# A linear attention and its routed experts: k scaled by cos with its relu, v and v*tan joined by one strided operand, all row writes on VectorE, and w1 loaded later

## The chip, the cores and the metric

The kernel runs on one core of a Trainium2 chip. The time is the device time of one launch, in microseconds; the figure of a kernel is the median of its runs. Engines are written as in the profile: PE is TensorE's matmul, PEld its weight load, DVE is VectorE, ACT is ScalarE, POOL is GpSimd, SP is SyncE. "L586" is line 586 of the kernel before.

## The reference

Two stages follow one another. The first is an attention without softmax, over 8 batches of 8 heads, 576 tokens and a head width of 64. Each token has an angle, theta, that grows with its position; `c` and `s` are its cosine and sine.

```python
def phi(x, c, s):
    r = np.maximum(x, 0.0)
    return np.concatenate([r * c, r * s], axis=-1)
q_p = phi(q, cos_w, sin_w)
k_p = phi(k, cos_w, sin_w)
kv = np.einsum('bhsf,bhsd->bhfd', k_p, v)
z = np.sum(k_p, axis=2)
num = np.einsum('bhsf,bhfd->bhsd', q_p, kv)
den = np.einsum('bhsf,bhf->bhs', q_p, z)[..., None] + 1e-06
return (num / den).astype(np.float32)
```

The 4608 resulting rows of 512 then go through a mixture of 8 experts:

```python
logits = x @ w_gate
expert_idx = np.argmax(logits, axis=1)
...
gate_w = probs[np.arange(N), expert_idx]
for i in range(N):
    e = expert_idx[i]
    if counts[e] < capacity:
        disp[e, counts[e]] = x[i]
...
h = np.maximum(np.einsum('ecd,edf->ecf', disp, w1), 0.0)
y = np.einsum('ecf,efd->ecd', h, w2)
...
        out[i] = gate_w[i] * y[expert_idx[i], pos[i]]
```

Each row takes one expert; w1 is 512 x 1024 and w2 1024 x 512 for each expert, and an expert takes at most 1152 rows.

## The kernel before

**Planner.** The kernel does not issue its work as it is written. Every piece of work is an `op` with an engine, an assumed cost, the data it reads and writes, the buffers it uses (`Ver`, a version that takes one of a fixed number of `Slots`) and a priority. `Plan.schedule` simulates the engines with those costs and fixes one order; `emit` writes the instructions in that order. `PHI` adds an offset to the priorities by kind of op. On the chip each engine runs its own list strictly in this order and waits wherever an input is late; the planner's costs say nothing of what the chip takes.

**Attention, for each batch.** `load` (L405, on SP's queue) brings v, k and q in two halves `u` of four heads each, 576 KB a load; a batch is six loads. `scale_v` (L433 on ACT, L435 on DVE) makes `vs`, which holds v times cos and v times sin for each of nine token groups `j`: 18 instructions a batch. `relu_k` (L419, in batch 0 L421) and `q_relu` (L458) clip k and q. `kv_half` (L504, the op KV) multiplies k by vs in tiles of 64x64 and sums over the tokens into PSUM. The result is copied twice by ACT: `kvt` (L516), which PE transposes (L533, op T), and `kva` (L521). The transposed copy `tsb` (L538) is multiplied with the gate weights `wg_sb` (L547, op G), and the products join `kva` (L552), so that one matmul later gives numerator, denominator and gate logits at once. q is transposed on PE (L468) and copied to `rq` (L475). The op P (L574), ten units a batch, multiplies `rq` by `kva`; each output row holds the cos part and the sin part. ACT copies the cos part to `tmp` (L581), and DVE adds tan of the position times the sin part (L586) to make `num`. Three PSUM buffers (`p`) pass from P to `tmp` and `num`.

**Routing, for each batch.** A chain of small DVE instructions (L627 to L735) makes the reciprocal of the denominator, the logits, the chosen expert (`oh`), its weight and, with counting matmuls on PE (L693 to L700) and a running `carry`, the place of each row; POOL adds a small number at L667. Then the five row groups of the batch are scaled and rounded to bf16 (`f_emit`, L758): groups 1 and 3 on POOL, 0, 2 and 4 on DVE. POOL scatters each group to DRAM with an indirect DMA (L767).

**Experts.** 43 blocks of 128 rows: a block is fetched (L967), transposed (L976), copied (`xT`, L982 on ACT or L984 on DVE), multiplied by one half of w1 (`up`, L999), clipped (`relu`, L1006), transposed back (L1014), copied (`hT`, L1020), and, after all blocks, multiplied by w2 (`down`, L1040), copied (`y`, L1046 and L1048) and scattered to the output (L1057). 20 blocks are taken from the first six batches, so that they can begin while the last batches are still at work. w1 and w2 are loaded by POOL's queue, which turns fp32 into bf16 on the way: the first half of w1 (`w1a`, L918) in eight loads that follow the KV of batches 0 to 5, the second half (`w1b`) and w2 after the attention has freed its memory.

The gate of the w1 loads is this line:

```python
w1_load(0, e, e + 0.1, ops_of("KV", 3 * e // 4))
```

Of the kernel before, what the change touches and what calls it, by code (L numbers as in the profile page):

```python
# [20 lines left out]
P = 128  # L21
DISJOINT = "the rows written are disjoint"
# [5 lines left out]
    "KV": 0.67, "P": 1.53, "Q": 1.08, "R": 0.18, "T": -0.18, "carry": 0.52, "count": -1.68, "down": 0.08,  # L28
    "end": 0.57, "fetch": 1.92, "gout": -0.13, "hT": 0.05, "ix": -0.43, "kvt": -0.86, "num": 0.22,
    "pad": -1.04, "pos": -0.01, "pre": -0.23, "relu": 0.14, "reluk": -0.5, "reluq": -1.78, "rq": -0.43,  # L30
    "seen": 0.24, "tab": 0.85, "tmp": 0.34, "tsb": 0.47, "turn": 5.12, "up": 2.21, "vs": -0.73, "w1": 0.14,
    "w2": 0.51, "wg": -1.23, "xg": 0.06, "xturn": -0.12,
# [25 lines left out]
class Plan:  # L58
# [6 lines left out]
    def op(self, eng, cost, fn, r=(), w=(), vers=(), prio=0.0, lat=0.1, mode=None, dma=0.0, after=()):  # L65
        o = Op()
        o.eng, o.cost, o.fn, o.prio, o.lat, o.mode, o.dma = eng, cost, fn, prio, lat, mode, dma
        o.seq, o.start, o.end = len(self.ops), None, None
# [18 lines left out]
    def schedule(self, window=0.25, switch=0.15, sticky=0.6):  # L87
# [11 lines left out]
        while done < len(self.ops):  # L99
            best = {}  # L100
            cands = []
            for o in ready:
                t = max(free.get(o.eng, 0.0), o.avail)
# [17 lines left out]
                if o.mode is not None and mode.get(o.eng) not in (None, o.mode):  # L121
                    t += switch
                cands.append((t, o))
                if o.eng not in best or t < best[o.eng]:
                    best[o.eng] = t
# [4 lines left out]
            eng = min(best, key=lambda e: best[e])  # L130
            t0 = best[eng]
            pick = None
            for t, o in cands:
                if o.eng == eng and t <= t0 + window:
                    pr = o.prio - (sticky if o.mode is not None and mode.get(eng) == o.mode else 0.0)
                    if pick is None or (pr, o.seq) < pick[0]:
                        pick = ((pr, o.seq), t, o)
            _, t, o = pick
# [29 lines left out]
    def emit(self):  # L168
        for o in self.order:
            o.fn()  # L170
# [3 lines left out]
def kernel(  # L174
# [11 lines left out]
    nc = tc.nc  # L186
# [24 lines left out]
    XT_ACT = 14  # L211
# [35 lines left out]
    kS, vS, qS = Slots("km", 4), Slots("vm", 2), Slots("qm", 2)  # L247
    qrS = Slots("qr", 2)
    vsS, rqS, kvaS = Slots("vs", 2), Slots("rq", 2), Slots("kva", 2)
    tmpS = Slots("tmp", 3)  # L250
    kvtS, tsbS, numS = Slots("kvt", 1), Slots("tsb", 1), Slots("num", 2)
# [6 lines left out]
    vs_t = [early.tile([P, HB, J, 2, D + 1], FP32, name=f"vs{i}") for i in range(vsS.n)]  # L258
# [23 lines left out]
    for t in range(2):  # L282
        nc.gpsimd.dma_start(out=wg_n[t * D:(t + 1) * D], in_=moe_w_gate.rearrange("(h d) e -> d h e", d=D))
# [16 lines left out]
    nc.scalar.activation(out=cosn[:], in_=tok_n[:], func=ACT.Sin, bias=halfpi[:])  # L300

# [20 lines left out]
    for t, tab in ((0, cosn), (1, sinn)):  # L322
      for vs in vs_t:
        nc.gpsimd.tensor_copy(out=vs[:, :, :, t, D], in_=tab[:].unsqueeze(1).to_broadcast([P, HB, J]))
    for t_ in num_t:
        nc.gpsimd.memset(t_[D:P, NJ, :, :], 1.0)

    nc.gpsimd.memset(wg_sb[:], 0.0)

    def wg_spread():  # L330
        for t in range(2):
            rows = slice(t * D, (t + 1) * D)
            for o in range(2):
                nc.gpsimd.tensor_copy(out=wg_sb[rows, 2 * o:2 * o + 2, t, :, :],
                                      in_=wg_n[rows].rearrange("p (u c o) e -> p o u c e", u=2, c=2)[:, o])
# [54 lines left out]
    def load(b, name, u):  # L390

        if name == "v":
            if u == 0:
                loaded[b, "v"] = Ver(vS)
            vm = loaded[b, "v"]
        else:
            vm = loaded[b, name, u] = Ver({"k": kS, "q": qS}[name])
        src = srcs[name][b].rearrange("(u c o) (p j) d -> u (o p) c (j d)", u=2, o=2, j=J)[u]

        def f():  # L400
            if name == "v":
                m = tl(vm, [P, HB, J, D], FP32, "early")[:, 2 * u:2 * u + 2, :, :]
            else:
                m = tl(vm, [P, 2, J, D], FP32, "early")[:]
            nc.sync.dma_start(out=m.rearrange("p c j d -> p c (j d)"), in_=src)  # L405
        op("SP", 0.5, f, w=[(name, b, u)], vers=[vm], prio=b - 1.2, dma=1.55).tag = ("load", name, b, u)
# [3 lines left out]
    def attention(b):  # L410

        vm = loaded[b, "v"]
        pr = float(b)

        def relu_k(u):
            def f():
                kk = loaded[b, "k", u].tile[:]
                if b:
                    nc.scalar.activation(out=kk, in_=kk, func=ACT.Relu)  # L419
                else:  # L420
                    nc.vector.tensor_scalar(out=kk, in0=kk, scalar1=0.0, scalar2=None, op0=ALU.max)  # L421
            return f


        vs = Ver(vsS)

        def scale_v(j, t, us):
            def f():
                tab = (cosn, sinn)[t]
                heads = slice(2 * us[0], 2 * us[-1] + 2)  # L430
                dst, src = vs_t[vs.slot][:, heads, j, t, 0:D], vm.tile[:, heads, j, :]
                if on_act(j):
                    nc.scalar.activation(out=dst, in_=src, func=ACT.Copy, scale=tab[:, j:j + 1])  # L433
                else:
                    nc.vector.tensor_scalar(out=dst, in0=src, scalar1=tab[:, j:j + 1], scalar2=None, op0=ALU.mult)  # L435
            return f

# [738 lines left out]
```

## Time and profile before

| | before |
|---|---|
| median of 3 runs | 396.09 us (395.18 to 398.47) |
| the profiled execution | 398.65 us |
| its span in the profile | 396.6 us |
| mean granted TensorE clock | 0.932 |
| busy: PE, DVE, ACT, POOL | 336.3, 210.2, 188.9, 154.3 us |

The span is what the profile's engines cover; the execution's own time lies 2.05 us above it. A row of a group reads: line, engine, operation, output and inputs with their shapes, count, then busy time and mean ns of one, then the engine's idle time before these instructions and what ended it. A row of waits reads: the waiting engine and line, what it waited for, total us, number of times, longest. Two rows of the same engine can overlap, as ACT and DVE start the next instruction before the last has ended: the means of the rows are longer than the distance from start to start.

### The profile page before, as it was taken

How to read it: one execution, taken by the hardware profiler on the slowest of the kernel's cores; microseconds unless marked ns; L12 is line 12 of the kernel's file. 1: busy time of each engine (PE TensorE's matmuls, PEld its weight loads, DVE VectorE, ACT ScalarE, POOL GpSimd, SP SyncE). 2: the span in 40 equal slices, each digit the busy share in tenths (PEclk: the TensorE clock that was granted, in tenths of full speed). 3: DMA queues.
4: the chain of work that ended last, by engine and by line, in shares of the span. 5: the costliest groups of instructions: out<-in, count | busy, mean ns of one | idle time of the engine just before them, and what ended most of it. 6: DMA issues, size and time to landing. Idle time of an engine off the chain costs nothing.

```text
span 396.6 us, 9673 instructions
## 1 busy us (share of the span) xinstructions
PE 336.3 (85%) x3368; PEld 221.2 (56%) x3368; DVE 210.2 (53%) x584; ACT 188.9 (48%) x403; POOL 154.3 (39%) x214
## 2 busy tenths in 40 slices
PE   6588698878897996788397787899999999999992
PEld 3477597757686875674254343455555544444440
DVE  6547878796867697878725333444333311222220
ACT  5576776777675695547063232345555311111110
POOL 6100546454653627084723222105000065555552
PEclk9978986999797799989879998999999999999998
DMA  8999787778979501126599997819920033342330
GB/s 271 335 341 311 246 248 225 240 223 260 259 221 229 197 3 62 45 71 147 172 202 236 202 213 146 176 47 165 211 51 2 1 134 159 139 162 110 126 129 1
DMA packets 38543, 66.63 MB, mean 168 GB/s; under 512 B 3903, under 2 KB 18655, under 8 KB 38498
## 3 DMA queue, kind: packets, MB, share of 16 engines
q0 software_dynamic: 18096, 31.00, 34.5%
q1 hardware_dynamic: 19250, 33.98, 26.1%
q10 hardware_dynamic: 1152, 1.05, 0.8%
q8 instruction: 29, 0.48, 0.5%
q14 instruction: 16, 0.13, 0.1%
HBM read 67.56 MB, written 17.06 MB: 213 GB/s over the span
## 4 chain that ended last, share of the span: by engine, by line
PE 44%; DVE 15%; DMA 12%; issue 11%; POOL 6%; ACT 5%; POOLq 2%; ACTq 2%; SPq 1%; DVEq 0%
PE p L999 17%; PE p L574 9%; PE p L1040 7%; POOL out_dram L1057 6%; DMA xr<-xd 5%; DMA vm<-in_v_dram 5%; PE a L1014 4%; DVE xg L758 4%; DVE num L586 3%; PE a L468 3%; DMA qm<-in_q_dram 2%; POOLq L1057 2%; ACT tmp L581 2%; PE a L976 2%; PE a L547 1%
## 5 line engine op out<-in xcount | busy, mean ns | idle before, releaser
L1006 ACT ACTIVATE h<-p 128x512 bf16<-128x512 f32 x86 | 51.3, 598 | 63.3 <-PE p L999 61.7
L1040 PE MATMUL p<-w,un 128*128 x344 | 74.6, 379 | 0.3 <-issue 0.3
L574 PE MATMUL p<-kva,rq 64*128 64x146 f32 x640 | 61.2, 345 | 13.9 <-DVE num L586 10.9
L1020 DVE COPY un<-a 128x512 bf16<-128x512 bf16 x86 | 36.0, 423 | 63.5 <-PE a L1014 63.3
L574 PEld LDWEIGHTS p<-kva,rq 64*128 64x128 f32 x640 | 53.1, 229 | 21.8 <-DVE num L586 14.5
L1040 PEld LDWEIGHTS <-un 128*128 128x128 bf16 x344 | 33.6, 98 | 40.6 <-issue 0.6
L586 DVE SCALAR_TENSOR_TENSOR num<-p,tant,tmp 128x292 f32<-128x292 f32 (+1 forms) x80 | 39.8, 516 | 24.4 <-ACT tmp L581 19.2
L767 POOL DMA_INDIRECT xd<-xg,si x40 | 47.1, 1178 | 11.1 <-issue 8.8
L999 PEld LDWEIGHTS <-un 128*128 128x128 bf16 x344 | 32.7, 99 | 30.5 <-issue 9.5
L999 PE MATMUL p<-w1a,un 128*128 x172 | 46.7, 399 | 2.5 <-POOL ids L971 0.5
L581 ACT COPY tmp<-p 128x292 f32<-128x292 f32 (+1 forms) x80 | 31.2, 402 | 35.3 <-PE p L574 25.8
L1048 DVE COPY y<-p 128x512 f32<-128x512 f32 x22 | 15.2, 691 | 57.7 <-PE p L1040 51.9
L999 PE MATMUL p<-w1b,un 128*128 x172 | 44.1, 378 | 0.0
L1057 POOL DMA_INDIRECT out_dram<-y,ids x20 | 19.5, 976 | 58.5 <-DVE y L1048 46.8
L504 PE MATMUL p<-vs,km 64*64 64x130 f32 x1152 | 34.6, 272 | 9.1 <-DVE km L421 4.3
L1046 ACT COPY y<-p 128x512 f32<-128x512 f32 x21 | 12.3, 586 | 61.2 <-PE p L1040 61.2
L504 PEld LDWEIGHTS p<-vs,km 64*64 64x64 f32 x1152 | 32.1, 133 | 11.2 <-issue 5.2
L1014 PEld LDWEIGHTS <-h 128*128 128x128 bf16 x344 | 25.2, 99 | 22.5 <-ACT h L1006 10.0
L1014 PE MATMUL a<-identb,h 128*128 128x128 bf16 x344 | 33.5, 222 | 4.9 <-ACT h L1006 4.2
L758 POOL TENSOR_TENSOR xg<-num,rden 128x512 bf16<-128x512 f32 x16 | 24.0, 1520 | 18.4 <-DVE rden L735 18.4
L971 POOL COPY ids<-xr 128x2 bf16<-128x2 bf16 x43 | 7.6, 190 | 56.6 <-DMA xr<-xd 56.3
L468 PE MATMUL a<-ident,qr 128*128 128x128 f32 x144 | 27.3, 319 | 2.1 <-ACT rq L475 1.8
(162 smaller groups left out, 405.2 us busy)
## 6 DMA issues: line engine op xcount, KB each, us to landing
vm<-in_v_dram SPq DMA_DIRECT2D x16, 576.0 KB
km<-in_k_dram SPq DMA_DIRECT2D x16, 576.0 KB
qm<-in_q_dram SPq DMA_DIRECT2D x16, 576.0 KB
w<-in_moe_w_dram POOLq DMA_DIRECT2D x16, 512.0 KB
xr<-xd SPq DMA_DIRECT2D x43, 128.5 KB
w1a<-in_moe_w_dram POOLq DMA_DIRECT2D x8, 512.0 KB
w1b<-in_moe_w_dram POOLq DMA_DIRECT2D x8, 512.0 KB
xd<-zrow ACTq DMA_DIRECT2D x8, 128.5 KB
```

The costliest lines, as they stand in the source:

```text
L468: nc.tensor.transpose(out=q_ps[:, n * P:(n + 1) * P], in_=qr.tile[:, j, :, :].rearrange("p c d -> p (c d)"), identity=ident[:])
L504: nc.tensor.matmul(out=kv_v[c * D:(c + 1) * D, o, u, :, :], lhsT=loaded[b, "k", u].tile[o * D:(o + 1) * D, c, j, :], rhs=vs_t[vs.slot][o * ...
L574: nc.tensor.matmul(out=p_ps[:, a, o, 0:2 * KW], lhsT=rq[u].tile[a * D:(a + 1) * D, o, col:col + P], rhs=kva.tile[a * D:(a + 1) * D, o, u, ...
L581: nc.scalar.copy(out=t[0:rows], in_=p_v[0:rows, :, 0:KW])
L586: nc.vector.scalar_tensor_tensor(out=num.tile[0:rows, c, u * HB:(u + 1) * HB, :], in0=p_v[0:rows, :, KW:2 * KW], scalar=tant[0:rows, c:c + ...
L758: eng.tensor_tensor(out=x[0:rows, c, 0:DT].rearrange("p (h d) -> p h d", h=H), in0=num.tile[0:rows, c, :, 0:D], in1=rv["rden"][0:rows, c, ...
L767: si = nc.gpsimd.indirect_dma_start(out=xd[:, :], out_offset=bass.IndirectOffsetOnAxis(ap=xg.si[0:rows, c:c + 1], axis=0), in_=xg.tile[0:r ...
L999: nc.tensor.matmul(out=hp, lhsT=xv.tile[:, g, :], rhs=w1h[m][:, bass.ds(e1, 1), g, :], start=(g == 0), stop=(g == G - 1))
L1006: nc.scalar.activation(out=h[:], in_=pvs[m].tile[:, 0, :].rearrange("p (g q i) -> p g i q", g=2, i=2), func=ACT.Relu)
L1014: nc.tensor.transpose(out=t_ps[:, x * P:(x + 1) * P], in_=hvs[m].tile[:, x // 2, x % 2, :], identity=identb[:])
L1040: nc.tensor.matmul(out=y_ps, lhsT=hts[x // G].tile[:, x % G, :], rhs=w2h[x // G][:, bass.ds(e2, 1), x % G, :], start=(x == 0), stop=(x == ...
L1057: oi = nc.gpsimd.indirect_dma_start(out=out[:, :], out_offset=bass.IndirectOffsetOnAxis(ap=idx, axis=0), in_=yv.tile[:], in_offset=None, b ...
```

## The change

- k is multiplied by cos in the same instruction that clips it (`scale_k`, 9 a batch), in place; v is multiplied only by tan (`scale_v`, 9 a batch). The matmul of KV then reads, as one operand of two pieces, 66 columns of v as loaded and 66 columns of v*tan; column 64 of the second piece holds ones and column 65 tan, for the denominators. v, and its product, lie in one tile for this.
- `kvt` is dropped: `kva` is kept with the cos and the sin part (t) as its innermost index, written by two copies, and is transposed directly. The gate weights are spread over the partitions to match. P's output so has both parts interleaved, and `tmp` and `num` read every second element.
- k has 2 buffers of a whole batch in place of 4 of half a batch, q 4 halves in place of 2, `rq` 3 in place of 2, `tmp` 4 in place of 3.
- All five row writes of a batch are on VectorE. The product before the logits' sum is stored transposed, so that the sum reads in order. The small addition on POOL becomes a ninth element of the sum.
- The planner may put an op on a second engine (`alt`, with a cost), for `k1`, `vt`, `rq`, `kva`, `tsb`, `gout`, `tmp`, `xT`, `relu`, `hT` and `y`. `PHI` has new values.
- The first half of w1 follows the KV of batches 4 to 7.

```diff
+        o.ways = [(eng, cost)] + ([alt] if alt else [])
...
-    kS, vS, qS = Slots("km", 4), Slots("vm", 2), Slots("qm", 2)
+    kS, vS, qS = Slots("km", 2), Slots("vm", 2), Slots("qm", 4)
-    vsS, rqS, kvaS = Slots("vs", 2), Slots("rq", 2), Slots("kva", 2)
-    tmpS = Slots("tmp", 3)
-    kvtS, tsbS, numS = Slots("kvt", 1), Slots("tsb", 1), Slots("num", 2)
+    vtS, rqS, kvaS = Slots("vt", 2), Slots("rq", 3), Slots("kva", 2)
+    tmpS = Slots("tmp", 4)
+    tsbS, numS = Slots("tsb", 1), Slots("num", 2)
...
+    for i in range(vtS.n):
+        nc.gpsimd.memset(v_tan(i)[:, :, :, D], 1.0)
+        nc.gpsimd.tensor_copy(out=v_tan(i)[:, :, :, D + 1], in_=tann[:].unsqueeze(1).to_broadcast([P, HB, J]))
...
+                nc.vector.tensor_scalar(out=wg_sb[:, 2 * o:2 * o + 2, t, :, :],
+                                        in0=wg_n[:].rearrange("p (u c o) e -> p o u c e", u=2, c=2)[:, o],
+                                        scalar1=of_t[:, t:t + 1], scalar2=None, op0=ALU.mult)
...
+                if eng == "ACT":
+                    nc.scalar.activation(out=kk, in_=kk, func=ACT.Relu, scale=cosn[:, j:j + 1])
                 else:
-                    nc.vector.tensor_scalar(out=kk, in0=kk, scalar1=0.0, scalar2=None, op0=ALU.max)
+                    nc.vector.tensor_scalar(out=kk, in0=kk, scalar1=0.0, scalar2=cosn[:, j:j + 1], op0=ALU.max,
+                                            op1=ALU.mult)
...
+                if eng == "ACT":
+                    nc.scalar.activation(out=dst, in_=src[:, :, :, j, :], func=ACT.Copy, scale=tann[:, j:j + 1])
                 else:
-                    nc.vector.tensor_scalar(out=dst, in0=src, scalar1=tab[:, j:j + 1], scalar2=None, op0=ALU.mult)
+                    nc.vector.tensor_scalar(out=dst, in0=src[:, :, :, j, :], scalar1=tann[:, j:j + 1], scalar2=None,
+                                            op0=ALU.mult)
...
+                            first = v_t[rows, v0:v0 + VX]
+                            both = bass.AP(first.tensor, first.offset, [tuple(first.ap[0]), (v1 - v0, 2), (1, VX)])
+                            nc.tensor.matmul(out=kv_v[c * D:(c + 1) * D, 2 * o + u, :, :],
+                                             lhsT=km.tile[rows, 2 * u + c, j, :], rhs=both,
                                              start=(j == 0), stop=(j == J - 1))
...
+            t = tl(kva, [P, 4, KW, 2], FP32, "early")
+            copy = nc.scalar.copy if eng == "ACT" else nc.vector.tensor_copy
+            copy(out=t[:, :, 0:D, :].rearrange("p w d t -> p w t d"), in_=kv_tile()[:, :, :, 0:D])
+            copy(out=t[:, :, D, :], in_=kv_tile()[:, :, 1, D:D + 2])
...
-                t = tl(tmp, [P, HB, KW], FP32, "early")
-                p_v = pv.tile[:].rearrange("p a (o x) -> p (a o) x", o=2)
-                nc.scalar.copy(out=t[0:rows], in_=p_v[0:rows, :, 0:KW])
+                (nc.scalar.copy if eng == "ACT" else nc.vector.tensor_copy)(out=t[0:rows], in_=by_t(0))
...
-                    out=num.tile[0:rows, c, u * HB:(u + 1) * HB, :], in0=p_v[0:rows, :, KW:2 * KW],
+                    out=num.tile[0:rows, c, u * HB:(u + 1) * HB, :], in0=by_t(1),
...
                 op("ACT", 0.33, g, r=[("pps", b, c, u)], w=[("tmp", b, c, u)], vers=[pv, tmp], prio=pr - 1,
-                   lat=0.15).tag = ("tmp", b, c, u)
+                   lat=0.15, alt=("DVE", 0.37)).tag = ("tmp", b, c, u)
...
-        for c in (1, 0, 3, 2, 4):
-            p_ = c in ON_POOL
-            op("POOL" if p_ else "DVE", 1.06 if p_ else 0.62, f_emit(c), r=[("rg", b), ("num", b)], w=[("xg", b, c)],
-               vers=[rt, xg, num], prio=pr).tag = ("xg", b, c)
+        for c0, c1 in ((0, 1), (1, 2), (2, 3), (3, 4), (NJ, NC)):
+            op("DVE", 0.62, f_emit(c0, c1), r=[("rg", b), ("num", b)], w=[("xg", b, c) for c in range(c0, c1)],
+               vers=[rt, xg, num], prio=pr).tag = ("xg", b, c0)
...
             op("ACT", 0.52, f_relu(m), r=[("h", i, m)], w=[("hr", i, m)], vers=[pvs[m], hvs[m]], prio=pm,
-               ).tag = ("relu", i, m)
+               alt=("DVE", 0.6)).tag = ("relu", i, m)
...
-            op("ACT" if i % 2 else "DVE", 0.52 if i % 2 else 0.63, f_y, r=[("yps", i)], w=[("y", i)], vers=[yp_, yv],
-               prio=pd - 3).tag = ("y", i)
+            op("ACT", 0.52, f_y, r=[("yps", i)], w=[("y", i)], vers=[yp_, yv], prio=pd - 3, alt=("DVE", 0.63)).tag = ("y", i)
...
-        w1_load(0, e, e + 0.1, ops_of("KV", 3 * e // 4))
+        w1_load(0, e, e + 0.1, ops_of("KV", min(4 + e // 2, B - 1)))
```

## The prediction

> **What bounds the kernel now.** I read the busy time by stages first, then the waits, then the timeline of three engines, and last the group rows, for prices. The stages (columns: stage, sum, busy time and instruction count of PE, PEld, DVE, ACT, POOL, then granted clock, DMA share, GB/s):
>
> ```profile
> 0.00:20.00 20.00, 12.53 (x180) 8.43 (x181) 12.07 (x63) 11.23 (x30) 7.70 (x28) 0.96 0.96 303
> 20.00:40.00 20.00, 16.45 (x250) 14.29 (x249) 12.40 (x34) 13.73 (x32) 0.10 (x1) 0.79 1.00 327
> 80.00:100.00 20.00, 15.62 (x281) 12.94 (x273) 16.18 (x42) 14.68 (x36) 10.29 (x10) 1.00 0.84 241
> 120.00:140.00 20.00, 16.62 (x176) 14.43 (x169) 14.00 (x37) 12.20 (x30) 10.72 (x10) 0.74 0.78 198
> 140.00:160.00 20.00, 15.75 (x293) 13.33 (x289) 16.00 (x43) 14.67 (x36) 9.46 (x9) 1.00 0.10 32
> 320.00:360.00 40.00, 40.00 (x187) 18.09 (x186) 7.97 (x12) 7.03 (x12) 22.32 (x23) 1.00 0.38 152
> ```
>
> The reader is to see three regimes. Up to 40 us the DMA engines are full. From 40 to 181 us no engine is full: PE, DVE and ACT are each busy 60 to 90%, tied together by one order. From about 200 us PE is nearly full; at 320 to 360 it is busy all the time. The change works on the first two.
>
> The routing of a batch begins with the instruction at line 627. It starts at 35.8, 57.1, 77.3, 97.3, 118.1, 140.7, 163.4 and 180.7 us, so the seven steps from batch 0 to batch 7 take 145 us, and the six after batch 1 take 20.6 us each. One batch's matmuls at the full clock, from the PE timeline: KV 4.24, Q 18 x 0.165 = 3.0, T 0.66, gates 1.08, P ten units at 0.60 (40 instructions took 3.09) = 6.0, counting 0.7. Sum 15.7. So 4.9 us of each step is not full-speed matmul: part is clock (the mean of the eight 20-us stages from 20 to 180 is 0.88), part is waiting. The waits of PE and DVE between 20 and 182 us (total, times, longest):
>
> ```profile
> PE p L574 <- DVE num L586: 10.9, 9, 2.9
> PE p L504 <- DVE num L586: 2.4, 2, 1.2
> PE a L533 <- ACT rq L475: 2.0, 6, 0.4
> PE a L533 <- ACT kvt L516: 1.0, 1, 1.0
> DVE num L586 <- ACT tmp L581: 19.2, 35, 1.7
> DVE vs L435 <- DMA vm<-in_v_dram: 7.9, 2, 4.9
> ```
>
> PE waits for VectorE's `num`, about 1.7 us a batch, and for ScalarE, about 0.7. The last line belongs to the DMA stage: VectorE stood 4.9 and 3.0 us waiting for v of batch 1, and PE's longest wait, 2.9 us until 31.5 us, is the second of these passed on. What filled the DMA engines then is seen in GpSimd's timeline and in the queue totals of 12 to 32 us (packets, MB, share of 16 engines):
>
> ```profile
> 9.90 1.63 POOL L918 DMA_DIRECT2D w1a<-in_moe_w_dram  x2
> q0 software_dynamic: 1056, 1.05, 30.9%
> ```
>
> Two loads of w1 (1 MB read for 0.5 MB written each) took 30.9% of 20 us, 6.2 us of DMA time, in front of the v that VectorE waited for.
>
> [...] The xg rows below agree: beside GpSimd's 1520 ns, VectorE's take 1115 and 1529 ns, and three end 0.6 us after GpSimd's two (3.60 against 3.00 us). [...] the lg sum reads 320 elements at a 32-byte step in 746 ns, the product before it reads the same number in order in 492. [...]
>
> **The change part by part.** The prices, count then busy us and mean ns:
>
> ```profile
> L433 ACT ACTIVATE vs<-vm,cosn 128x256 f32<-128x256 f32 x35 | 18.2, 520 | 1.9 <-DMA vm<-in_v_dram 1.9
> L435 DVE TENSOR_SCALAR vs<-vm,cosn 128x256 f32<-128x256 f32 x28 | 9.6, 343 | 7.9 <-DMA vm<-in_v_dram 7.9
> L419 ACT ACTIVATE km<-km 128x1152 f32<-128x1152 f32 x14 | 16.4, 1169 | 0.9 <-DMA km<-in_k_dram 0.9
> L516 ACT COPY kvt<-p 128x512 f32<-128x512 f32 x8 | 4.6, 571 | 7.3 <-PE p L504 7.3
> L758 POOL TENSOR_TENSOR xg<-num,rden 128x512 bf16<-128x512 f32 x16 | 24.0, 1520 | 18.4 <-DVE rden L735 18.4
> L758 DVE TENSOR_TENSOR xg<-num,rden 128x512 bf16<-128x512 f32 x16 | 17.2, 1115 | 0.3
> L586 DVE SCALAR_TENSOR_TENSOR num<-p,tant,tmp 128x292 f32<-128x292 f32 x64 | 32.0, 517 | 19.8 <-ACT tmp L581 17.8 <-issue 1.7
> L638 DVE TENSOR_REDUCE lg<-lg 128x40 f32<-128x320 f32 x8 | 6.0, 746 | 0.3
> L1006 ACT ACTIVATE h<-p 128x512 bf16<-128x512 f32 x86 | 51.3, 598 | 63.3 <-PE p L999 61.7
> L1046 ACT COPY y<-p 128x512 f32<-128x512 f32 x21 | 12.3, 586 | 61.2 <-PE p L1040 61.2
> ```
>
> *Scaling.* Eighteen `vs` become nine `k1` and nine `vt` of the same 128x256: equal. The two relus go, 2 x 1.06 us of ScalarE start to start. *kv.* `kvt` goes (0.5 us start to start); one copy of 8 columns comes, taken as 0.2, the row of the 64x64 gate copies. T now waits for `kva` with that copy, 0.2 us later after KV. Together ScalarE loses 2.4 us of its 14.7 in 20. The moving operand grows from 130 to 132 columns, 1.5% of 4.24 us: 0.06 us a batch. That it joins two places of one tile no row shows; both halves run in order, so I take nothing (to +0.3 us).
>
> *Row writes.* Three VectorE writes under contention, 3.6 us, become five at 0.6, 3.0. GpSimd loses 3.0 us, and the hop at line 667. lg sums in order: 746 becomes about 400, and its product writes at a 32-byte step (0 to +0.33 us, taken +0.15). VectorE gains 0.8 us a batch.
>
> *Strided PSUM reads.* `tmp` and `num` read every second fp32. For ScalarE the trace answers: line 1006 reads PSUM at that step, 598 ns, line 1046 in order, 586. For VectorE nothing does[...]. I take nothing: [...] the planner's price for a relu on VectorE with this step (0.60) is not above that of the plain y copy (0.63), which ran in 691 ns. The other end is the slower rival.
>
> *w1 late.* The early DMA share goes: of the 7.9 us waited I take 5.5 (3 to 8), since PE still has P of batch 0 to do. q's buffers go from two to four, so its loads queue sooner on SP; k and v slots now live until KV has read them, but SP's loads of a batch, 3.54 MB or 10 to 11 us at 330 GB/s, fit in a step. All eight w1 loads, 0.84 us each of GpSimd's queue, fall behind KV of batches 4 to 7, beside the last q, k and v; four fell between 94 and 122 us before, the same density. The last two come after KV of batch 7, 163 us before and about 146 here, when DMA is at 0.1 to 0.2: past row scatters (5 x 1.29 us at most), two issues and 3 us of transfer, 157 us. The first matmul on w1a was at 178.8 and would be near 160. Covered, by 3 us at the worst.
>
> *Prologue.* Some nine small VectorE instructions of 0.15 to 0.2 us, wg_spread's four among them; half 1 of batch 0 waits for v until 9.1 us anyway, which hides most: +0.3 (0 to 1.5).
>
> *What the freed time buys in a step.* The PE waits on VectorE and ScalarE are 1.7 and 0.7 us. Giving ScalarE's freed 2.4 us work that was VectorE's should end three quarters of the first and half of the second, 1.65; the clock should give 0.55 of the roughly 2 us it costs[...]. I take 2.2 (0 to 3.5), 13.2 over six steps. *Tail.* The last routing gets 0.6 + 0.35 shorter, scatters begin 2.4 us sooner, but PE waits on VectorE's table: -1.0 (0 to -2.5). *Experts.* Free choice of engine for xT, relu, hT and y lies beside a full PE: 0 (+-3). If that cover were gone, a y copy on the other engine costs 0.1 us.
>
> Sum: -5.5 + 0.3 - 13.2 - 1.0 = -19.4 us. The profiled execution took 398.65 us, 2.05 more than its span of 396.6; 398.65 - 19.4 = 379.3. The median shown is 2.56 below that execution, so the forecast for the median is 377 us.
>
> **The rivals.** (1) *The step does not shorten.* The chain inside a batch (KV, copy, T, copy, gates, copy, P, routing), not engine load, sets 20.6 us; only the DMA stage and the tail gain, -6.2: 390 us. For it: VectorE waits 19.2 us for tmp while ScalarE is a quarter idle. Against: PE's own waits end at VectorE. (2) *w1 too late.* The first expert matmuls stand until w1 lands and take back what was won: 396. For it: w1's matmuls wait for all eight loads. Against: DMA is idle at that time. (3) *Slower: VectorE pays for strided PSUM.* `num` becomes 0.82, +3.0 us a batch; `tmp` copies that the planner sends to VectorE at its price of 0.37 take 0.67, five of them 3.4. VectorE's 16 us become 16 - 0.8 + 3.0 + 3.4 = 21.6, plus its remaining waits of about 1.5: steps of 23.1, +2.5 x 7 = 17.5, less the early 5.5: +12, 408 us. It decides where VectorE's work passes 20.6 us a batch, that is where the extra is over about 0.23 us for each of these fifteen.
>
> **How the numbers follow.** Forecast 0.60 (own range 367 to 388), rival 1 0.17, rival 2 0.07, rival 3 0.16. About 1% is what a measurement of this kernel can tell from no change. Faster by more: 0.60 and most of rival 1, 0.74. Within 1%: 0.10. Slower: 0.16. The low end is all gains at their bounds, -8 - 21 - 2.5 - 3 = -34.5, 362; the high end, 400, takes in rivals 1 and 2 and the mildest of rival 3.
>
> **What would show it.** Right: the first routing instruction of the batches (line 627 of before) starting every 18 to 18.5 us; its first near 30 us; no v wait above 1 us before 35 us; PE waits on `num` under half; `num` at 0.52. Wrong: steps of 20 us and more, `num` near 0.8, or a gap on PE ended by w1a.

## The result, and the profile after

The changed kernel took 409.25 us (median of 4 runs, 408.31 to 411.46) beside 397.17 us for the kernel before. The ratio is 1.0317, with a 95% interval of 1.0247 to 1.0386: slower by 3%, where 377 us was forecast. The profiled execution took 411.46 us, its span was 409.7.

The stages first (columns as in the prediction):

```profile
0.00:20.00 20.00, 7.04 (x48) 3.58 (x52) 12.48 (x72) 6.97 (x21) 5.21 (x25) 0.74 0.94 339
20.00:40.00 20.00, 16.14 (x204) 14.33 (x197) 6.84 (x17) 9.86 (x25) 0.00 (x0) 0.76 0.74 250
80.00:100.00 20.00, 13.70 (x223) 11.34 (x223) 9.88 (x27) 9.93 (x24) 3.80 (x4) 0.83 0.44 139
120.00:140.00 20.00, 15.17 (x250) 13.02 (x250) 12.77 (x28) 11.28 (x28) 7.64 (x8) 0.91 0.96 269
320.00:360.00 40.00, 39.84 (x208) 18.97 (x206) 3.66 (x8) 14.71 (x25) 16.64 (x17) 1.00 0.28 106
```

PE's first 20 us hold 7.04 us of work where they held 12.53, and at 80 to 100 PE, DVE and ACT are all idler than before. The expert stage (last line) is as full as it was. So the time was lost in the attention, and not to an engine that became full.

The first instruction of the routing (line 662 now) starts at 44.2, 69.6, 89.7, 114.6, 133.7, 158.4, 181.5 and 195.6 us. Batch 0 is 8.4 us later than before, and the steps are 25.4, 20.1, 24.8, 19.2, 24.7, 23.1 and 14.1. Up to batch 5 they alternate: those that end with batches 1, 3 and 5 are long, those with 2 and 4 short. PE's timeline shows why. These are all matmuls of KV up to batch 3 (start, duration; in brackets idle time before and what ended it):

```profile
18.11 6.71 PE L539 MATMUL p<-v,km 64*64 64x132 f32 x144 [11.76 <-DMA km<-in_k_dram]
43.13 2.26 PE L539 MATMUL p<-v,km 64*64 64x132 f32 x72
48.18 2.26 PE L539 MATMUL p<-v,km 64*64 64x132 f32 x72 [2.80 <-ACT v L467]
68.53 4.29 PE L539 MATMUL p<-v,km 64*64 64x132 f32 x144
88.60 2.26 PE L539 MATMUL p<-v,km 64*64 64x132 f32 x72
93.72 3.25 PE L539 MATMUL p<-v,km 64*64 64x132 f32 x72 [2.85 <-ACT v L467]
```

In the kernel before, KV of batches 0 and 1 looked like this:

```profile
7.54 2.23 PE L504 MATMUL p<-vs,km 64*64 64x130 f32 x72 [1.90 <-DVE km L421]
12.15 2.23 PE L504 MATMUL p<-vs,km 64*64 64x130 f32 x72 [2.38 <-DVE km L421]
35.57 4.24 PE L504 MATMUL p<-vs,km 64*64 64x130 f32 x144
```

The changed kernel's first KV waits 11.76 us for a DMA. But the last of its own inputs was ready at 11.46, when VectorE ended its scalings of batch 0. What landed at 18 us belongs to batch 1: the row names a load of k, but VectorE, which starts on batch 1 at the same moment, had waited for v:

```profile
10.40 1.06 DVE L458 TENSOR_SCALAR km<-km,cosn 128x128 f32<-128x128 f32 x5
17.94 0.74 DVE L469 TENSOR_SCALAR v<-v,tann 128x256 f32<-128x256 f32 x2 [2.04 <-DMA v<-in_v_dram]
```

In batches 1, 3 and 5 KV stops between its halves for ScalarE's `v` writes, which are those of the next batch. The rest of the batch hangs on that stop: in batch 1 ScalarE writes five pieces of `v` at 45.45 after waiting for KV's first half, stands until 50.57 for the second half, and only then reaches the exponential of batch 0's routing, on which VectorE waits, and behind VectorE PE. First ScalarE, then VectorE, then PE:

```profile
45.45 2.68 ACT L467 ACTIVATE v<-v,tann 128x256 f32<-128x256 f32 x5 [1.81 <-PE p L539]
50.57 1.59 ACT L467 ACTIVATE v<-v,tann 128x256 f32<-128x256 f32 x3 [2.44 <-PE p L539]
53.48 0.24 ACT L685 ACTIVATE ex<-dl 128x40 f32<-128x40 f32 x1
53.75 0.20 DVE L701 TENSOR_REDUCE gate<-ex 128x5 f32<-128x45 f32 x1 [6.39 <-ACT ex L685]
55.14 1.09 PE L563 MATMUL a<-ident,kva 128*128 128x128 f32 x4 [3.74 <-DVE pos L747]
```

The waits between 20 and 196 us (total, times, longest), those that are new:

```profile
DVE gate L701 <- ACT ex L685: 18.3, 6, 6.4
ACT v L467 <- PE p L539: 13.8, 6, 3.4
DVE v L469 <- ACT v L467: 12.6, 3, 11.4
PE a L563 <- DVE pos L747: 8.6, 5, 3.7
PE p L539 <- ACT v L467: 8.5, 3, 2.9
PE p L607 <- DVE num L621: 2.3, 5, 0.7
```

The last is the one that the prediction set out to shorten, 10.9 us before: it did shrink. Waits on `v` took its place.

**Theory A.** The joined operand of KV begins in v of the batch's slot and ends in its v*tan. In the tile the order is v slot 0, v slot 1, v*tan slot 0, v*tan slot 1. If the ordering of instructions takes such an operand for all that lies between its ends, KV of an even batch counts as reading v slot 1, and KV of an odd batch as reading v*tan slot 0, both of the next batch. Rival B: the new order on the engines and the free choice of engine cost the time. Rival C: reading two places of a tile is slow in itself.

### The profile page after: what moved, and what is told of

It reads as the page before. It is cut to its first block, busy times and chain, and to the rows that moved or that the text cites. A ratio compares the mean times of both kernels' runs of the same rounds, so it can differ in the third digit from the quotient of the medians.

```text
span 409.7 us, 9580 instructions
## 1 busy us (share of the span) xinstructions
PE 338.8 (83%) x3368; PEld 223.2 (54%) x3368; DVE 182.3 (44%) x541; ACT 210.2 (51%) x455; POOL 127.1 (31%) x189
## 3 DMA queue, kind: packets, MB, share of 16 engines
q1 hardware_dynamic: 19250, 33.98, 25.4%
## 4 chain that ended last, share of the span: by engine, by line
PE 41%; issue 13%; ACT 12%; DMA 9%; POOL 8%; DVE 7%; POOLq 6%; SPq 1%; ACTq 0%
PE p L1027 15%; PE p L607 7%; DMA xr<-xd 6%; PE p L539 6%; POOL out_dram L1085 5%; POOLq L1085 5%; ACT v L467 4%; PE a L1045 4%; DVE num L621 3%; PE a L497 3%; DMA km<-in_k_dram 3%; PE a L577 2%; POOL xd L800 2%; ACT km L456 2%; ACT tmp L617 2%
## 5 line engine op out<-in xcount | busy, mean ns | idle before, releaser
L1036 ACT ACTIVATE h<-p 128x512 bf16<-128x512 f32 x78 | 46.6, 598 | 48.0 <-PE p L1027 42.9
L607 PE MATMUL p<-kva,rq 64*128 64x146 f32 x640 | 58.6, 333 | 4.2 <-DVE num L621 2.3
L539 PE MATMUL p<-v,km 64*64 64x132 f32 x1152 | 39.7, 290 | 22.5 <-DMA km<-in_k_dram 11.8
L607 PEld LDWEIGHTS p<-kva,rq 64*128 64x128 f32 x640 | 50.5, 219 | 11.9 <-DVE num L621 6.6
L1051 DVE COPY un<-a 128x512 bf16<-128x512 bf16 x69 | 29.2, 423 | 48.7 <-PE a L1045 48.3
L539 PEld LDWEIGHTS p<-v,km 64*64 64x64 f32 x1152 | 35.9, 142 | 25.8 <-issue 15.3
L1076 ACT COPY y<-p 128x512 f32<-128x512 f32 x42 | 24.6, 585 | 48.0 <-PE p L1071 48.0
L467 ACT ACTIVATE v<-v,tann 128x256 f32<-128x256 f32 (+1 forms) x62 | 30.1, 495 | 16.4 <-PE p L539 13.8
L1045 PEld LDWEIGHTS <-h 128*128 128x128 bf16 x344 | 25.4, 99 | 20.3 <-ACT h L1036 4.7
L497 PE MATMUL a<-ident,qr 128*128 128x128 f32 x144 | 29.4, 334 | 4.1 <-ACT km L456 3.1
L456 ACT ACTIVATE km<-km,cosn 128x256 f32<-128x256 f32 (+1 forms) x66 | 27.9, 484 | 0.3 <-DMA km<-in_k_dram 0.3
L1085 POOL DMA_INDIRECT out_dram<-y,ix x23 | 22.3, 970 | 16.9 <-ACT y L1076 16.6
```

What stands on the lines that cost most here:

```text
L467: nc.scalar.activation(out=dst, in_=src[:, :, :, j, :], func=ACT.Copy, scale=tann[:, j:j + 1])
L497: nc.tensor.transpose(out=q_ps[:, n * P:(n + 1) * P], in_=qr.tile[:, j, :, :].rearrange("p c d -> p (c d)"), identity=ident[:])
L539: nc.tensor.matmul(out=kv_v[c * D:(c + 1) * D, 2 * o + u, :, :], lhsT=km.tile[rows, 2 * u + c, j, :], rhs=both, start=(j == 0), stop=(j == ...
L607: nc.tensor.matmul(out=p_ps[:, a, o, 0:2 * KW], lhsT=rq[u].tile[a * D:(a + 1) * D, o, col:col + P], rhs=kva.tile[a * D:(a + 1) * D, 2 * o ...
L1036: nc.scalar.activation(out=h[:], in_=src, func=ACT.Relu)
L1045: nc.tensor.transpose(out=t_ps[:, x * P:(x + 1) * P], in_=hvs[m].tile[:, x // 2, x % 2, :], identity=identb[:])
```

## The experiments

The kernel before took 398 to 399 us in the first and third set of runs, 386 to 387 in the second and fourth, so times are compared within a set, or as ratios to the kernel before in it. Even a ratio does not carry over exactly: the kernel of run 5 took 0.9956 of the kernel before in the second set and 0.9731 in the third.

Runs 1, 2, 7 and 10 keep the changed kernel's order of work on every engine (run 7 has two matmuls for each one of KV, run 10 leaves out two fills at the start). In runs 3, 4, 5, 6, 8 and 11, and in the changed kernel with w1 early, the edit made the planner order the work anew, so each of them changes two things at once.

**1. v and v*tan of a half side by side** (first set). The instructions, their sizes and their order on every engine are the same.

```diff
-    VT0 = vS.n * 2 * VH
-    v_t = early.tile([P, VT0 + vtS.n * HB * J * VX], FP32, name="v")
+    VG = VH + 2 * J * VX
+    v_t = early.tile([P, vS.n * 2 * VG], FP32, name="v")
...
-                        v0 = vm.slot * 2 * VH + u * VH + (c * J + j) * D
-                        v1 = VT0 + ((vt.slot * HB + 2 * u + c) * J + j) * VX
+                        v0 = (vm.slot * 2 + u) * VG + (c * J + j) * D
+                        v1 = (vt.slot * 2 + u) * VG + VH + (c * J + j) * VX
```

> The changed kernel with one thing different: inside the same tile, v and v*tan of one slot and half lie side by side, so that the joined operand spans nothing but its own half. Instructions, their order and all sizes stay. Theory A (in the order v, v, v*tan, v*tan the joined operand spans another batch's slot and is ordered against it): KV of batch 0 starts near 11.5 us and not at 18.1, the stops of 2.8 us between the halves of KV in batches 1, 3, 5 go, steps between routings are even at 18.5 to 20.5 us, first routing near 36 us, the whole 380 to 392 us. Rival B (the planned order and the free choice of engine are what costs): steps stay near 25 and 19 by turns, 405 to 411. Rival C (reading two places of a tile is slow in itself): KV and steps keep their time, only the first KV may start sooner, above 402.

Measured: 382.8 us, 0.9628 of the kernel before (0.9549 to 0.9707). PE's timeline, KV of batches 0 to 2:

```profile
7.16 0.44 PE L541 MATMUL p<-v,km 64*64 64x132 f32 x4 [0.66 <-ACT km L458]
8.77 4.27 PE L541 MATMUL p<-v,km 64*64 64x132 f32 x140 [1.17 <-DVE v L471]
31.67 4.29 PE L541 MATMUL p<-v,km 64*64 64x132 f32 x144
52.77 4.29 PE L541 MATMUL p<-v,km 64*64 64x132 f32 x144
```

The first KV starts at 7.2 and runs on from 8.8 us, no stop is left between the halves, first routing is at 32.8, and the six steps from batch 1 to 7 take 18.8 us each. KV itself takes what it took: rival C falls, and with it B as the cause of the loss, since the order is the changed kernel's. The program that each kernel builds names the wait itself: ahead of its first KV matmul the changed kernel's PE waits for the seventh and the ninth of SP's loads, the two halves of v of batch 1; in the side by side layout it waits for neither.

**2. The slots of v*tan swapped** (first set): v0, v1, v*tan1, v*tan0.

```diff
-                        v1 = VT0 + ((vt.slot * HB + 2 * u + c) * J + j) * VX
+                        v1 = VT0 + (((1 - vt.slot) * HB + 2 * u + c) * J + j) * VX
```

> The changed kernel with the two slots of v*tan in the other order (v0, v1, v*tan1, v*tan0). Theory A: now the joined operand of batches 0, 2, 4, 6 spans both slots of the other parity and that of batches 1, 3, 5, 7 spans none of a coming batch; KV of batch 0 still waits until about 18 us, and the long steps (24 to 25 us) become those that end with the routing of batches 2, 4 and 6 in place of 1, 3 and 5. Total 403 to 413 us. Rival B (planned order) and rival C (the joined read itself): the long steps stay at 1, 3 and 5, 409 us.

Measured: 411.3 us, one run. The first KV and the stop of batch 2:

```profile
18.04 6.53 PE L539 MATMUL p<-v,km 64*64 64x132 f32 x144 [11.90 <-DMA v<-in_v_dram]
40.36 4.29 PE L539 MATMUL p<-v,km 64*64 64x132 f32 x144
61.38 2.26 PE L539 MATMUL p<-v,km 64*64 64x132 f32 x72
66.89 3.92 PE L539 MATMUL p<-v,km 64*64 64x132 f32 x72 [3.25 <-ACT v L467]
```

The stops moved to batches 2, 4 and 6, and batches 1, 3 and 5 have none for `v` of another batch. Steps: 23.1, 24.0, 16.8, 24.4, 21.5, 29.4, 14.6. A layout that differs in nothing but an address moves the stops as theory A says.

**3. Late w1 alone, in the kernel before** (first set); its gate becomes `ops_of("KV", min(4 + e // 2, B - 1))`.

> The kernel before with only the gate of the w1 loads moved (after KV of batches 4, 4, 5, 5, 6, 6, 7, 7). My term for this part was -5.5 us (-3 to -8): expected 391 (388 to 394), first routing at 30 to 32 us in place of 35.8, and no gap of the expert matmuls ended by w1a. Rival: the time won early is given back in later steps or by w1 landing too late, 395 to 399.

Measured: 395.77 us, 0.9947 (0.9921 to 0.9974). The first routing came at 31.04 in place of 35.78, the last at 174.7 in place of 180.7, so 4.7 us were won early and 6.0 by the last routing. From there to the end it took 219.4 us against 215.9: 3.5 were given back. PE's stage of 180 to 200 us has a granted clock of 0.74, where it was 0.89, and its waits for rows fetched (`xr`) after 165 us are 6.9 us, where they were 1.8. Neither was tested as the cause. The expected 391 us did not come; the rival's 395 to 399 did: what was won early was in part given back, though no gap on PE was ended by w1a.

**4. Side by side, w1 early** (first set), with the gate `ops_of("KV", 3 * e // 4)`.

> The side by side layout with the gate of w1 as in the kernel before. If late w1 is worth its 5.5 us only where the first KV is not held by something else, this is 4 to 6 us slower than the side by side layout with w1 late. Rival: with a shorter prologue the DMA engines are not the limit, within 1 us of it. Theory A's own expectation against the changed kernel: still 10 us or more faster.

Measured: 393.79 us, 0.9886 (0.9857 to 0.9915), 11.0 above the side by side layout; more than expected. In the profiles it is 7.7 us: the first routing is 5.9 later (38.64 against 32.78), the seven steps are 3.8 shorter (130.1 against 133.9), and the time behind the last routing is 5.7 longer (220.4 against 214.7). Only the first of these is where the w1 loads stood; the others come together with a new order.

**5. Side by side, row writes shared with GpSimd** (second set, and third with the side by side layout beside it); `ON_POOL` is (1, 3).

```diff
+                eng = nc.gpsimd if c0 in ON_POOL else nc.vector
-        for c0, c1 in ((0, 1), (1, 2), (2, 3), (3, 4), (NJ, NC)):
+        for c0, c1 in ((1, 2), (0, 1), (3, 4), (2, 3), (NJ, NC)):
```

> The side by side layout with the row writes of token groups 1 and 3 on GpSimd again, in the old order. My sum gave the row writes on VectorE 0.6 us a batch in the steps and 0.6 of the tail: expected 4 to 6 us slower than the side by side layout (387 to 389). Rival: the rows are not on the path that sets the steps, within 2 us of it (381 to 385). The pairs of writes on VectorE and GpSimd should take 1.1 and 1.5 us each again.

> Shared row writes in the side by side layout, now with the side by side layout beside it. In its first profile the seven routing steps took 131.6 us, against 133.9 with all rows on VectorE, so the rows gained nothing there; what was behind the last routing took 5.8 us more. Expected 1 to 5 us slower than the side by side layout run beside it; my sum said 4.2 and put it in the steps. Within 1 us if the time behind the last routing was chance.

Measured: 386.26 (0.9956) in the second set; in the third 388.50 beside 385.77, so 2.7 us slower. Its seven steps took 135.3 us beside 139.5, and the time behind the last routing 220.1 beside 212.1. The writes took 1005 and 1223 ns on the two engines against 686 on VectorE alone. So the row writes gain nothing in the steps, where my sum had them. The kernel with shared writes loses behind the last routing, as every kernel with an order planned anew does (see below); that the writes do it is not shown. In the second set the side by side layout was not run, so its 386.26 us answers neither expectation.

**6. Side by side, k in four half buffers** (second set), `Slots("km", 4)` and scaling by halves.

> The side by side layout with k in four buffers of a half each, as before, and k scaled by halves (18 instructions a batch in place of 9; on ScalarE 0.39 us in place of 0.50 each, 2.5 us more a batch if all are there). If whole buffers of k hold its loads back enough to matter, 376 to 381. Rival, which I think likelier: loads are not what sets the steps once the first v has come, and the extra instructions cost 0 to 1.2 us a batch: 383 to 392.

Measured: 389.36 us, but from 382.8 to 393.8 over four runs, so no interval. The side by side layout was not run in this set. In the fourth, where the kernel before stood alike, all four of its runs (372.0 to 375.7) are below the lowest of these, but that comparison is between sets, and the order is a new one. Nothing speaks for half buffers; what whole ones cost stays open.

**7. The operand taken apart, in the changed kernel's layout** (second set).

```diff
-                            nc.tensor.matmul(out=kv_v[c * D:(c + 1) * D, 2 * o + u, :, :],
-                                             lhsT=km.tile[rows, 2 * u + c, j, :], rhs=both,
+                            at = (v0, v1)[t]
+                            nc.tensor.matmul(out=kv_v[c * D:(c + 1) * D, 2 * o + u, t, :],
+                                             lhsT=km.tile[rows, 2 * u + c, j, :], rhs=v_t[rows, at:at + VX],
```

> The changed kernel in its own layout (v, v, v*tan, v*tan), with the joined operand taken apart: one matmul of 66 columns on v and one on v*tan, 288 a batch in place of 144 of 132 columns. Theory A: neither reaches over another slot, so KV of batch 0 starts near 11.5 us, and the stops between the halves of KV go in all batches; against that KV itself takes longer, from 4.3 to between 4.3 and 8.6 us a batch. Expected 385 to 405 us, with no alternation of 25 and 19 us. If the order on the engines were the cause, first KV at 18 us and 25/19 stay and the total is 409 to 430.

Measured: 395.84 us, one run, the kernel before 387.4. First KV at 7.45 with eight matmuls and from 9.26 with the rest, first routing at 35.8 in place of 44.2, no stop for `v` of another batch; the steps are 18.9, 18.8, 21.8, 17.0, 21.8, 30.9 and 13.9. A half of KV, now 144 matmuls, in batch 6:

```profile
154.54 2.34 PE L538 MATMUL p<-v,km 64*64 64x66 f32 x144
158.01 2.60 PE L538 MATMUL p<-v,km 64*64 64x66 f32 x144
```

Joined, a half took 2.26 us. So joining saves 0.1 to 0.3 us a half where PE runs through. From 20 to 170 us this kernel also has gaps between KV's own matmuls that the profile lays to no releaser:

```profile
PE p L538 <- issue: 15.8, 8, 4.6
```

They stay open. So does what taking the operand apart is worth in all: 395.84 is within the expected range, but that was written for a kernel before at 398 us, and neither the changed kernel nor the side by side layout was run in this set.

**8. Side by side, engines fixed as before** (second set).

> The side by side layout without the planner's free choice of engine: each copy and scaling goes to the engine that the kernel before named for it (odd token groups and group 4 of k and v on ScalarE, the rest on VectorE; expert copies as before). My sum gave the choice nothing in the experts (within 3 us) and did not price it in the attention. Expected 380 to 388, near the side by side layout. If the choice is what made room for VectorE, 390 and above.

Measured: 397.07 us, 1.0262 (1.0193 to 1.0330). In its profile `v` writes of VectorE and ScalarE wait for each other, 4.4 and 4.3 us, which led to runs 10 and 11.

**9. The changed kernel and the side by side layout again, and the changed kernel with w1 early** (third set).

> The changed kernel itself, as the measure for the runs beside it: between the first two sets of runs the kernel before went from 398.0 to 387.4 us, so times of different sets can't be set against each other. Theory A: its first KV ends its wait near 18 us and its steps alternate whatever the condition, so it stays 2.5 to 4% above the kernel before.

> The side by side layout again, beside the changed kernel and the shared row writes. Theory A: 5.5 to 7% under the changed kernel (0.930 to 0.945 of it) and below the kernel before by 2.5 to 4.5%, whatever the condition of the chip. If its gain belonged to the first set only, within 1% of the kernel before.

> The changed kernel in its own layout with the gate of w1 as before the change. Theory A: KV of batch 0 waits for v of batch 1, which now lands behind the early w1 loads; first routing at 46 to 52 us in place of 44.2, alternation as in the changed kernel, total 2 to 8 us above the changed kernel run beside it. If DMA is not what the first KV waits for, within 1 us of it.

Measured: 412.22 (1.0300, 1.0238 to 1.0361), 385.77 (0.9638, 0.9586 to 0.9690) and 416.43 (1.0387, 1.0322 to 1.0453). The side by side layout is 0.936 of the changed kernel. With w1 early the first KV waits until 23.07 us, against 18.03 in the changed kernel beside it, and the first routing comes at 47.7: batch 0's KV is tied to batch 1's load.

```profile
23.07 6.14 PE L539 MATMUL p<-v,km 64*64 64x132 f32 x144 [16.58 <-DMA v<-in_v_dram]
```

The total, 4.2 us longer, is less sure: the runs of the two kernels overlap (411.8 to 419.2 and 409.7 to 416.6).

**10 and 11. One uniform step over the heads, and the same with the engines fixed** (fourth set). v and v*tan of a head lie together.

```diff
-                dst = v_tan(vt.slot)[:, 2 * us[0]:2 * us[-1] + 2, j, 0:D].rearrange("p (u c) d -> p u c d", c=2)
+                dst = v_tan(vt.slot)[:, heads, j, 0:D]
...
-                        v0 = vm.slot * 2 * VH + u * VH + (c * J + j) * D
-                        v1 = VT0 + ((vt.slot * HB + 2 * u + c) * J + j) * VX
+                        v0 = (vm.slot * HB + 2 * u + c) * VH + j * D
+                        v1 = (vt.slot * HB + 2 * u + c) * VH + J * D + j * VX
```

> The side by side layout taken one step further: v and v*tan of one head lie together, so that a scaling touches four pieces with one uniform step. Theory A in its wider form (an operand of several pieces in a shared tile is ordered against all that its span covers): the waits of VectorE's and ScalarE's v*tan writes for each other (4.3 us in the side by side layout) go to nothing, KV of batch 0 starts at 8.8 us or before, and the whole gains 0 to 4 us on the side by side layout run beside it (0.990 to 1.000 of it). Rival: these waits lie beside other work, within 1 us.

> The layout by head with the engine of each copy and scaling fixed as in the kernel before. In the side by side layout this took 397.1 us, with 8.7 us of mutual waits. If those waits are what made it slow, it comes within 2 us of the layout by head with the free choice (380 to 386). If the fixed shares are what is slow (VectorE 208 us busy against 182, and VectorE releases most waits), 388 to 396.

> The side by side layout as the measure for the two runs beside it: 381 to 387 us, 0.955 to 0.970 of the kernel before if that takes about 398, and nearer to 1 if the kernel before is in the condition in which it took 387.

Measured: by head 366.26 us, 0.9502 of the kernel before (0.9392 to 0.9612); with engines fixed 391.08 (1.0119, 1.0000 to 1.0238); side by side 374.50 (0.9714, 0.9611 to 0.9816). The stages of the layout by head:

```profile
0.00:20.00 20.00, 14.45 (x179) 9.90 (x180) 13.07 (x76) 9.40 (x27) 5.17 (x23) 0.91 0.93 336
80.00:100.00 20.00, 19.17 (x409) 16.89 (x409) 17.56 (x46) 17.85 (x47) 8.20 (x9) 1.00 0.95 285
120.00:140.00 20.00, 19.13 (x314) 16.63 (x315) 17.42 (x55) 11.30 (x30) 8.48 (x8) 1.00 0.38 72
```

In the side by side layout of this set, writes of `v*tan` wait for each other across the engines; by head these waits are gone. The first two lines are side by side; then seven such writes of ScalarE in a row, first side by side, then by head:

```profile
ACT v L469 <- DVE v L471: 2.6, 3, 1.3
DVE v L471 <- ACT v L469: 1.8, 3, 0.6
70.09 3.77 ACT L469 ACTIVATE v<-v,tann 128x256 f32<-128x256 f32 x7
65.10 2.90 ACT L467 ACTIVATE v<-v,tann 128x256 f32<-128x256 f32 x7
```

It is 8.2 us faster than the side by side layout (0.978 of it), where 0 to 4 was expected: the six steps after batch 1 take 16.4 us beside 18.3. The rival, that the waits lie beside other work, falls. The waits between the engines are 4.4 us, half of the gain. The expectation had left out that these writes were ordered on one engine as well: side by side each starts when the one before has ended, 0.54 us apart, and by head 0.40 us apart. Over the 54 of them on ScalarE that is 27.6 us busy against 23.5. These 4.1 us and the 4.4 come near the 8.2; that they are the gain was not tested by itself. KV of batch 0 missed its 8.8 us: all but eight of its matmuls start at 10.56, after VectorE's scaling of k. In the layout by head PE, DVE and ACT are all fuller at 80 to 100 us than in the kernel before or the changed one. This is the version to keep: 5% under the kernel before.

With the engines fixed the waits are gone too, and it still takes 24.8 us more, so the waits were not the main thing that made run 8 slow. Its order was planned anew for these shares, with priorities that belong to the free choice, so the 24.8 are choice and order together; in the profiles it is 26.2, of which 2.5 lie ahead of the first routing, 15.6 in the steps and 8.0 behind the last routing.

## Why the prediction was wrong

**The step that failed** is the one on the joined operand: "That it joins two places of one tile no row shows; both halves run in order, so I take nothing (to +0.3 us)." I priced the read and not the order that it brings. The read was right: KV takes 4.29 us a batch, 4.24 before. The order cost 409 - 383 = 26 us: in the profiles, 11.5 us until the first routing (44.24 against 32.78), 17.5 over the seven steps (151.4 against 133.9), and 0.6 less after it. In the third set, where both kernels were run, it was 26.5. With it fell my "k and v slots now live until KV has read them, but SP's loads of a batch ... fit in a step": the loads fit, but KV stood waiting for one of them. The layout of the tile stood in the diff, and the question was which other batch lies between the two ends.

The rest of the sum was too good as well: with the false order gone the kernel is 15.2, 13.7 and 12.0 us under the kernel before in the three sets that have both, where the sum had 19.4.

**Early DMA, -5.5.** The size at its place was right: with late w1 the first routing comes 4.7 us sooner in the kernel before (run 3) and 5.9 side by side (run 4). What it is worth at the end the runs do not price. Late w1 took 2.2 us less in the kernel before and 11.0 less side by side, but each time with a new order, and 4.2 less in the changed kernel, where the runs overlap.

**What a new order costs.** One pattern runs through the profiles. From the last routing to the end, every kernel whose order was planned anew took 219.4 to 225.3 us, whatever had been changed in it; every kernel with the changed kernel's order took 209.9 to 215.1, and the kernel before 215.9. The priorities in `PHI` were not set anew for these edits. So part of what runs 3, 4, 5, 8 and 11 show may belong to the order and not to the edit, and no run separates the two.

**The steps, -2.2 each.** PE's wait for `num` fell from 10.9 to 2.3 us, as the prediction's last part asked. Freed of the false order, the steps after batch 1 were 18.8, 19.7 and 18.3 us in the three sets, against 20.6 in the one profile of the kernel before; the forecast was 18.4. By head they were 16.4. The share laid to the clock, 0.55 us a step, hardly came: over the eight stages from 20 to 180 us the mean granted clock was 0.88 before, 0.85 in the changed kernel and 0.89 side by side.

**Scaling, equal.** Mis-sized in the joined tile: ScalarE's writes of `v*tan` start 0.54 us apart there, 0.40 by head (run 10).

**Row writes.** Five in a row took 3.09 us, forecast 3.0. A write of 128x512 took 686 ns and one of 64x512 677, where in the kernel before, with GpSimd's writes beside them, they took 1115 and 1529. My 0.6 us a write was an estimate, from the 3.60 us of VectorE's three beside the 3.00 of GpSimd's two. But run 5 finds nothing of it in the steps.

```profile
56.13 3.09 DVE L790 TENSOR_TENSOR xg<-num,rden 128x512 bf16<-128x512 f32 x5
```

**lg:** the product went from 492 to 745 ns, the sum from 746 to 486. Each handles 320 elements, and the one that has the 32-byte step took 746 ns before and 745 after, the one in order 492 and 486; so the two changes cancel. My figures for both were estimates: I had 0.15 us more for the first, and it was 0.25; for the second I had about 400 ns, and it was 486.

**Strided PSUM, nothing.** Right, and the slower rival with it is refuted: its sign came, its mechanism did not. The rows (the last is of the kernel before):

```profile
L621 DVE SCALAR_TENSOR_TENSOR num<-p,tant,tmp 128x292 f32<-128x292 f32 x64 | 32.4, 519 | 17.2 <-ACT tmp L617 12.1 <-issue 4.7 <-ACT rq L504 0.5
L1038 DVE TENSOR_SCALAR h<-p 128x512 bf16<-128x512 f32 x8 | 5.4, 688 | 4.2 <-PE p L1027 2.9 <-PE a L1045 1.2 <-issue 0.2
L1076 DVE COPY y<-p 128x512 f32<-128x512 f32 x1 | 0.7, 692 | 1.6 <-PE p L1071 1.6
L669 DVE TENSOR_TENSOR lg<-num,rden 128x320 f32<-128x320 f32 x8 | 6.0, 745 | 0.3
L674 DVE TENSOR_REDUCE lg<-lg 128x40 f32<-128x320 f32 x8 | 3.9, 486 | 0.3
L634 DVE TENSOR_TENSOR lg<-num,rden 128x320 f32<-128x320 f32 x8 | 3.9, 492 | 0.3
```

`num` at an 8-byte step takes 519 ns, in order 517; the relu at that step 688, the plain copy 692 (691 in the kernel before, over 22). The rival's 0.30 us more for each `num` was an estimate that no row of the kernel before showed; measured, it is 2 ns.

**Free choice of engine, nothing in the experts.** Mis-sized as a whole: I let the freed time of ScalarE take over VectorE's work at 1.65 us a step, and had no term for what the planner's order is worth in the attention. Run 11 puts choice and order together at 24.8 us in the layout by head. **Tail, -1.0:** from the last routing to the end 215.9 us before, 214.1 after, 214.7 side by side. **w1 too late:** neither in the changed kernel nor in run 3 was a gap on PE ended by w1a; that rival falls.

That the layout by head ends at 0.950, where 377 of 396 is 0.952, is partly chance: it is another layout than the one forecast, in a set where the kernel before took 386 us; the row writes gave the steps nothing of what the sum had for them, and the choice of engine and the order may have given what the sum had no term for.

## What to carry to other kernels

Before an operand is joined from two places of a tile, write down what lies between its ends and who writes it when: it can be ordered against all of that, across buffers and across batches, as here at a cost of 26 us. Lay what is read together side by side (here 409 to 383 us), with one uniform step (8.2 us more), and look in the timeline for a wait whose own inputs had been ready, as KV's were at 11.46 us and it started at 18.11. Routing steps that alternated with the parity of a double buffer, about 25 and 19 us, pointed here to its slots. And where a planner sets the order, compare only programs with the same order, or count the new order as a second change.

## What had not been expected of the hardware

The kernel before took 398.0 and 399.4 us in two sets of runs and 387.4 and 386.5 in two others, and the side by side layout moved with it (382.8, 385.8, then 374.5). The mean granted clock of the kernel before was between 0.92 and 0.97 in both kinds of set, so the clock doesn't tell them apart. Nor does the chip alone: the first two sets, 398.0 and 387.4, ran on one and the same chip, the other two on two others. The cause is open. And 144 matmuls of 66 columns, each with its own weights, took 2.34 to 2.60 us where 72 of 132 took 2.26.
